# Two-branch gated attention on one core: the start of the projections, with all of x loaded at once and two q blocks taken per portion

## The chip, the cores and the metric

The kernel runs on one core of one Trainium2 chip. The metric is the device time of one execution in microseconds (us). Lower is better. Three runs of the kernel before gave 2798.04, 2798.07 and 2798.45 us, median 2798.07 us. One further execution was taken with the profiler.

## The reference, cut to what matters

Two attention blocks, A and B, see the same input `x` and have their own weights. A gate worked out from `x` mixes their outputs.

```python
# B = 1, S = 2048 tokens, D = 512, H = 32 heads, Dh = 16
def block(x, wqkv, wo):
    q, k, v = split_heads(x @ wqkv)                 # [D, 3D]: q, k, v
    p = softmax(q @ k.T * Dh ** -0.5)               # full, per head
    return merge_heads(p @ v) @ wo
g = sigmoid((x * gate_w).sum(-1, keepdims=True))
out = g * block(x, wqkv_a, wo_a) + (1 - g) * block(x, wqkv_b, wo_b)
```

The outermost part of this that matters here is `x @ wqkv`. It is done with every float32 operand split into a high part (rounded to the `float32r` format) and a low part (the rest), so that a product takes three matmuls: high by high, low by high, high by low.

## The kernel before, in words

The program is written engine by engine in a fixed order (`manual_schedule`): each engine takes its instructions in the order of the code, and waits on semaphores for what it reads and for buffers that must come free. The engines are TensorE (PE, with PEld for its weight loads), ScalarE (ACT), VectorE (DVE), GpSimd (POOL) and SyncE (SP), which issues nearly all DMAs.

The work falls in two stages.

1. **Projections**, about the first 300 us. `x` comes in transposed, `xT` [512, 2048], in four **portions** of 512 tokens. A portion is one tile `raw` of 128 x 4 x 512 float32 (1 MB): four pieces of 128 rows of `xT`, k = 0 to 3. `split_x` makes `xh` (ACT, a cast) and `xl` (DVE, a subtraction) from it; these stay for the whole stage. The columns of `wqkv` for q and k are taken in 16 **blocks** of 128 columns: for each branch s and each group g of 8 heads, one block of q and one of k. `load_w` fetches a block's weights (`wraw`, 256 KB, three buffers) and `split_w` makes `whi` (ACT) and `wlo` (DVE), two buffers each.
2. **Attention**, the other 2500 us: scores, row maxima, exponentials and sums for 64 heads, with the output projections between them. The change doesn't touch it.

`project_qk` works a block: for each of the four portions it makes one **tile** of 128 x 512 in a PSUM bank `ps_st` (four banks in rotation) by 12 matmuls (L251): `whi` by `xh` for k = 0 to 3, then `wlo` by `xh`, then `whi` by `xl`. ACT copies the tile's high part to `part0` (L254), DVE subtracts for `part1` (L255). Two tiles fill a `part` pair of 128 x 1024, two pairs in rotation. Two DMAs of 512 KB then write a pair to memory, to `qd` or `kd` (L257). For the first half of a k block, DVE and POOL work out a further remainder and SP writes it to `xd` (L261 to L267).

At the start, SP issues the first block's weights, the first portion in four pieces, the second portion in two, and the second block's weights. `raw` has two buffers, so the loads of the third and fourth portion (L230) stand on SP behind waits for the splits of the first and second (`split_x`, L236 on ACT and L237 on DVE). All four `split_x` stand on ACT and DVE ahead of the second block's `split_w` and of the first block's evictions. Then the blocks run one after the other: q of group 0, k of group 0, q of group 1, k of group 1, and so on. At the head of block i, SP gets the weights of block i + 3, and ACT and DVE split those of block i + 1.

`vpool` holds two tiles `vg` of 128 x 16 x 8 x 17 float32, each 2176 elements a partition, where a portion has 2048. They are first filled with v by `load_v` on POOL's queue, after block 9.

Of the kernel before, what the change touches and what calls it, by code (L numbers as in the profile page):

```python
# [51 lines left out]
def gated_mha(ctx: ExitStack, tc: tile.TileContext, xT, x, wqkv_a, wo_a, wqkv_b, wo_b, gate_w, out):  # L52
    nc = tc.nc
    pe, act, dve, pool = nc.tensor, nc.scalar, nc.vector, nc.gpsimd
# [7 lines left out]
    ps_st = ctx.enter_context(tc.tile_pool(name="ps_st", bufs=4, space=PSUM))  # L62
# [6 lines left out]
    xd = [[dram.tile([2, HG, DH, 512], F32, name=f"xd{s}{g}") for g in range(NG)] for s in range(2)]  # L69
# [111 lines left out]
    pt = {}  # L181
# [13 lines left out]
    vpool = ctx.enter_context(tc.tile_pool(name="vpool", bufs=2))  # L195
    vg = {}
# [9 lines left out]
    with tc.tile_pool(name="xs", bufs=1) as xs, tc.tile_pool(name="pro", bufs=2) as pro:  # L206
        xh = [xs.tile([P, KC, 512], F32R, name=f"xh{c}") for c in range(NQ)]
        xl = [xs.tile([P, KC, 512], F32R, name=f"xl{c}") for c in range(NQ)]
        wblocks = {}

        raws = {}

        def load_w(s, col, n):
            raw = pro.tile([P, KC, n], F32, name="raw" if n == 512 else "wraw", bufs=2 if n == 512 else 3)
            nc.sync.dma_start(raw, wqkv[s][:, col:col + n].rearrange("(k p) c -> p k c", p=P))
            raws[s, col] = raw

        def split_w(s, col, n):
            raw = raws.pop((s, col))
            tag, bufs = ("wv", 1) if n == 512 else ("w", 2)  # L220
            hi = pro.tile([P, KC, n], F32R, name=f"{tag}hi", bufs=bufs)
            lo = pro.tile([P, KC, n], F32R, name=f"{tag}lo", bufs=bufs)
            act.copy(hi, raw)
            dve.tensor_tensor(lo, raw, hi.bitcast(F32), op=ALU.subtract)
            wblocks[s, col] = (hi, lo)

        def load_x(c, n):
            raw = pro.tile([P, KC, 512], F32, name="raw")
            for k in range(0, KC, n):
                nc.sync.dma_start(raw[:, k:k + n], xT[k * P:(k + n) * P, c * 512:(c + 1) * 512].rearrange(  # L230
                    "(k p) t -> p k t", p=P))
            return raw

        def split_x(c, n, raw):
            for k in range(0, KC, n):
                act.copy(xh[c][:, k:k + n], raw[:, k:k + n])  # L236
                dve.tensor_tensor(xl[c][:, k:k + n], raw[:, k:k + n], xh[c][:, k:k + n].bitcast(F32),  # L237
                                  op=ALU.subtract)

        def project_qk(s, g, isk, between):  # L240
            hi, lo = wblocks.pop((s, isk * DM + g * P))
            dst = (kd if isk else qd)[s][g]
            for half in range(2):
                pt = [pro.tile([P, 1024], F32R, name=f"part{i}") for i in range(2)]
                for c in range(2):
                    cc = half * 2 + c
                    ps = ps_st.tile([P, 512], F32, name="ps_st")
                    n = 0
                    for a, b in ((hi, xh[cc]), (lo, xh[cc]), (hi, xl[cc])):
                        for k in range(KC):  # L250
                            pe.matmul(ps, a[:, k], b[:, k], start=n == 0, stop=n == 3 * KC - 1)  # L251
                            n += 1
                    sl = slice(c * 512, (c + 1) * 512)
                    act.copy(pt[0][:, sl], ps)  # L254
                    dve.tensor_tensor(pt[1][:, sl], ps, pt[0][:, sl].bitcast(F32), op=ALU.subtract)  # L255
                for i in range(2):
                    nc.sync.dma_start(dst[i].rearrange("h d t -> (h d) t")[:, half * 1024:(half + 1) * 1024],  # L257
                                      pt[i].bitcast(F32))
                if isk and half == 0:
                    d = pro.tile([P, 512], F32, name="rise_k", bufs=1)  # L260
                    dve.tensor_tensor(d, ps, pt[0][:, :512].bitcast(F32), op=ALU.subtract)  # L261
                    pool.tensor_tensor(d, d, pt[1][:, :512].bitcast(F32), op=ALU.subtract)
                    dt = [pro.tile([P, 512], F32R, name=f"rise_p{i}", bufs=1) for i in range(2)]
                    pool.tensor_copy(dt[0], d)
                    pool.tensor_tensor(dt[1], d, dt[0].bitcast(F32), op=ALU.subtract)
                    for i in range(2):
                        nc.sync.dma_start(xd[s][g][i].rearrange("h d t -> (h d) t"), dt[i].bitcast(F32))  # L267
                between()

        v_st = [const.tile([P, H, 17], F32, name=f"v_st{i}") for i in range(2)]  # L270
        for t in v_st:
            pool.memset(t[:, :, 16:17], 1.0)

        def project_v(s, t):
            hi, lo = wblocks[s, 2 * DM]
            c, o = divmod(t * P, 512)
            ps = ps_st.tile([P, 512], F32, name="ps_st")
            n = 0
            for a, b in ((xh[c], hi), (xl[c], hi), (xh[c], lo)):
                for k in range(KC):  # L280
# [12 lines left out]

        block(load_w, 0)
        x0 = load_x(0, 1)
        block(split_w, 0)
        split_x(0, 1, x0)
        for c in range(1, NQ):
            split_x(c, 2, load_x(c, 2))
            if c < 3:  # L300
                block(load_w, c)
        ahead = [(m, c) for m in range(NT + LEAD + 2) for c in range(4)]

        def run_ahead():
            turn[0] = 0
            for _ in range(min(3, len(ahead))):
                m, c = ahead.pop(0)
                max_plain(m, c)
                if (m, c) == (NT - 1, 3):
                    max_split(0)  # L310
                    pending.append(0)

        pending = []
        for i, (s, g, isk) in enumerate(blocks):
            block(split_w, i + 1)
            block(load_w, i + 3)
# [4 lines left out]
            project_qk(s, g, isk, run_ahead if i >= 8 else lambda: None)  # L321
# [136 lines left out]
    banks, fill_only = [], []  # L458
# [166 lines left out]
    for r in range(2, ROUNDS, 2):  # L625
        h, kt = divmod(r, NT)
# [69 lines left out]
```

## Time and profile before

| what | value |
|---|---|
| median of three runs | 2798.07 us (2798.04 to 2798.45) |
| profiled execution, its own time | 2798.53 us |
| its span, first to last instruction | 2796.8 us |
| mean granted TensorE clock | 0.999 |
| PE busy | 2781.7 us (99%) |
| ACT busy | 2424.0 us (87%) |
| DVE busy | 2363.1 us (84%) |
| POOL busy | 254.8 us (9%) |
| DMA, mean | 81 GB/s |

The span is 1.73 us shorter than the execution's own time: that much lies around the instructions. In the profile, `L251` is the line of the kernel that issued an instruction, `out<-in` names its tiles without their numbers, and `x4` says that four instructions of a kind are merged in a row. The busy time of a matmul is modelled and includes the time in which its results drain, so the pace of matmuls is read from their starts, not from their durations. "PE 98%" in the chain of work that ended last means that nearly all of the span is a chain of matmuls. The clock column gives the granted TensorE clock as a share of full speed.

### The profile page before, as it was taken

To read this page: it belongs to the slowest core of one execution; us is meant where nothing else is said; L and a number is where in the kernel's file an instruction comes from. 1 tells how busy PE (TensorE), PEld (TensorE's weight loads), DVE (VectorE), ACT (ScalarE), POOL (GpSimd) and SP (SyncE) were. 2 spreads that over 40 slices of the span, in tenths; PEclk is the share of its full clock that TensorE was granted. 3 is DMA by queue.
4 is the path that set the end of the run, shared out by engine and by line. 5 is a ranking of instruction groups with operands and counts; after the bars stand their busy time and mean duration, and the time that the engine had idled before them with its cause. 6 is when DMAs were issued, how large, how long until landed. Compare 5 with 4: busy or idle time off the path is not lost.

```text
span 2796.8 us, 65495 instructions
## 1 busy us (share of the span) xinstructions
PE 2781.7 (99%) x26176; PEld 1317.1 (47%) x26176; DVE 2363.1 (84%) x4431; ACT 2424.0 (87%) x4789; POOL 254.8 (9%) x456
## 2 busy tenths in 40 slices
PE   8999999999999999999999999999999999999999
PEld 7877544444444444444444445444444444444444
DVE  4155799999999999999999877899999999998774
ACT  3221799999999999999999977899999999998785
POOL 2010112110000000000100232000000001011201
PEclk9999999999999999999999999999999999999999
DMA  7673423333333223333432442332323333333302
GB/s 259 203 247 146 96 60 79 66 68 58 70 62 55 53 60 56 58 60 58 89 58 49 102 102 61 58 58 50 63 53 60 58 78 70 58 73 87 76 11 93
DMA packets 91126, 225.25 MB, mean 81 GB/s; under 512 B 24150, under 2 KB 34358, under 8 KB 78278
## 3 DMA queue, kind: packets, MB, share of 16 engines
q1 hardware_dynamic: 88262, 212.15, 34.0%
q0 software_dynamic: 2560, 8.91, 1.2%
q8 instruction: 206, 3.38, 0.5%
q14 instruction: 98, 0.80, 0.1%
HBM read 152.07 MB, written 68.94 MB: 79 GB/s over the span
## 4 chain that ended last, share of the span: by engine, by line
PE 98%; ACT 1%; DMA 0%; DVE 0%; SPq 0%; issue 0%
PE acc L589 38%; PE ps_m L140 26%; PE ps_st L191 13%; PE ps_st L140 8%; PE ps_st L251 6%; PE ps_st L281 3%; PE ps_m L475 3%; ACT p L193 1%; DMA raw<-in_xT 0%; PE ps_st L475 0%; PE ps_st L526 0%; PE ps_m L526 0%; DVE o_acc L527 0%; PE ps_m L513 0%; SPq L230 0%
## 5 line engine op out<-in xcount | busy, mean ns | idle before, releaser
L193 ACT ACTIVATE p<-ps_st 128x512 f32<-128x512 f32 x4088 | 2073.0, 626 | 82.7 <-PE ps_st L191 69.7
L145 DVE TENSOR_REDUCE mxp<-ps_m 128x1 f32<-128x512 f32 x3096 | 1949.8, 683 | 184.5 <-PE ps_st L191 135.2
L140 PE MATMUL ps_m<-k_st,q_st 48*128 48x512 f32 x3596 | 1353.9, 446 | 0.1
L191 PE MATMUL ps_st<-q_st,k_st 50*128 50x512 f32 x4096 | 1215.6, 426 | 0.0
L589 PE MATMUL acc<-p,vg 128*17 128x384 f32 (+1 forms) x16336 | 1182.8, 384 | 2.9 <-ACT ev L597 2.0
L140 PEld LDWEIGHTS ps_m<-k_st,q_st 48*128 48x128 f32 x3596 | 608.6, 183 | 550.0 <-DVE mxp L145 499.7
L191 PEld LDWEIGHTS ps_st<-q_st,k_st 50*128 50x128 f32 x4096 | 617.3, 184 | 200.3 <-ACT p L193 179.8
L589 PEld LDWEIGHTS acc<-p,vg 128*17 128x17 f32 x16336 | 313.9, 96 | 422.4 <-issue 399.6
L157 DVE CUSTOM_DVE_ANT_0 rise<-ps_m,rise 128x512 f32<-128x512 f32 x500 | 339.6, 679 | 0.0
L152 ACT ACTIVATE rise<-ps_st 128x512 f32<-128x512 f32 x500 | 301.8, 604 | 37.3
L140 PE MATMUL ps_st<-x_st,q_st 48*128 48x512 f32 x500 | 248.1, 496 | 0.0
L140 PEld LDWEIGHTS ps_st<-x_st,q_st 48*128 48x128 f32 x500 | 91.4, 183 | 211.6 <-ACT p L193 211.1
L167 POOL CAST mparts<-mrow 128x16 fp32r<-128x16 f32 x64 | 12.6, 197 | 1913.8 <-DVE mrow L166 1913.8
L254 ACT CAST part<-ps_st 128x512 fp32r<-128x512 f32 x64 | 37.4, 587 | 131.9 <-PE ps_st L251 117.0
L255 DVE TENSOR_TENSOR part<-ps_st,part 128x512 fp32r<-128x512 f32 x64 | 43.9, 690 | 90.3 <-ACT part L254 79.3
L475 PE MATMUL ps_m<-wo,ot 128*128 128x512 f32 (+1 forms) x354 | 91.0, 402 | 0.0
L284 ACT COPY v_st<-ps_st 128x512 f32<-128x512 f32 x32 | 18.8, 587 | 79.8 <-PE ps_st L281 70.3
L251 PE MATMUL ps_st<-xh,whi 128*128 128x512 f32 x256 | 73.0, 405 | 8.1 <-ACT xh L236 8.1
L475 PEld LDWEIGHTS ps_m<-wo,ot 128*128 128x128 f32 (+1 forms) x354 | 64.0, 188 | 20.3 <-DVE mxp L157 5.9
L251 PE MATMUL ps_st<-xh,wlo 128*128 128x512 f32 x256 | 69.9, 396 | 0.0
L251 PE MATMUL ps_st<-xl,whi 128*128 128x512 f32 x256 | 69.5, 394 | 0.0
L251 PEld LDWEIGHTS ps_st<-xh,whi 128*128 128x128 f32 x256 | 47.6, 191 | 24.7 <-ACT xh L236 10.4
(95 smaller groups left out, 814.4 us busy)
## 6 DMA issues: line engine op xcount, KB each, us to landing
k_st<-kd SPq DMA_DIRECT2D x128, 256.0 KB
q_st<-qd SPq DMA_DIRECT2D x128, 256.0 KB
qd<-part SPq DMA_DIRECT2D x32, 512.0 KB
kd<-part SPq DMA_DIRECT2D x32, 512.0 KB
k_st<-kd SPq DMA_DIRECT2D x128, 128.0 KB
q_st<-qd SPq DMA_DIRECT2D x128, 128.0 KB
od<-ev SPq DMA_DIRECT2D x63, 256.0 KB
vd<-v_st SPq DMA_DIRECT2D x32, 272.0 KB
```

Source lines behind the costliest of these rows:

```text
L140: pe.matmul(ps, q[b:b + SC, t * P:(t + 1) * P], k, start=True, stop=True)
L145: dve.tensor_reduce(o[:, c:c + 1], ps, op=ALU.max, axis=AX.X)
L152: act.activation(rises[m], ps, AF.Relu)
L157: dve.tensor_tensor_reduce(out=rise, in0=ps, in1=rise, scale=1.0, scalar=LOWEST, op0=ALU.add, op1=ALU.max, accum_out=o[:, 0:1])
L191: pe.matmul(ps, k[b:b + SC + 2, kk * P:(kk + 1) * P], q[b:b + SC + 2, cc * 512:(cc + 1) * 512], start=True, stop=True)
L193: act.activation(pt[r][:, c * 512:(c + 1) * 512], ps, AF.Exp, scale=SCALE)
L251: pe.matmul(ps, a[:, k], b[:, k], start=n == 0, stop=n == 3 * KC - 1)
L254: act.copy(pt[0][:, sl], ps)
L255: dve.tensor_tensor(pt[1][:, sl], ps, pt[0][:, sl].bitcast(F32), op=ALU.subtract)
L281: pe.matmul(ps, a[:, k, o:o + P], b[:, k], start=n == 0, stop=n == 3 * KC - 1)
L475: pe.matmul(ps, ot[a][:n, slot, sl], wt[b][:n, g], start=G == groups[0] and i == 0, stop=G == groups[-1] and i == 2)
L589: pe.matmul(acc[32 * c:32 * c + 17, qa * P:qb * P], v[:, 4 * a + c if final else kt, j], p[:, c * 512 + qa * P:c * 512 + qb * P], start=fi ...
```

## The change

Three things are changed at the start of the projections.

- **Loads.** `load_x` puts portions 0 and 1 into `raw` as before, and portions 2 and 3 into the two `vg` tiles of `vpool`. SP issues all of it ahead of anything else: the first block's weights, portion 0, the second block's weights, portions 1 to 3, the third block's weights. The weights of the fourth block, which SP issued ahead of the first write before, and those of the fifth now come after the writes of the first two blocks.
- **Order of the blocks.** The second and third change places: q of group 0, q of group 1, k of group 0, k of group 1, then as before.
- **Shared portions.** The first two blocks no longer run one after the other. For each portion, PE makes the tile of block 0 and that of block 1, ACT and DVE split the next portion, and then evict the two tiles. On portion 0, each of these two tiles goes piece by piece: for k = 0 to 3, high by high, low by high, high by low. The third block's `split_w` stands between the last evictions of the two blocks. `project_qk` is cut into `qk_tile` (matmuls) and `qk_parts` (eviction and writes); from the third block on they are called as before.

The diff, cut to its core:

```diff
         def load_x(c, n):
-            raw = pro.tile([P, KC, 512], F32, name="raw")
+            if c < 2:
+                raw = pro.tile([P, KC, 512], F32, name="raw")
+            else:
+                raw = vpool.tile([P, NT, HG, 17], F32, name="vg").rearrange("p k h d -> p (k h d)")
+                raw = raw[:, :KC * 512].rearrange("p (k t) -> p k t", k=KC)
...
+        PARTS = ((0, 0), (1, 0), (0, 1))
...
+        def qk_tile(i, cc):
...
+            steps = [(k, p) for k in range(KC) for p in PARTS] if cc == 0 and i < 2 else \
+                [(k, p) for p in PARTS for k in range(KC)]
+            for n, (k, (a, b)) in enumerate(steps):
+                pe.matmul(ps, w[a][:, k], (xh, xl)[b][cc][:, k], start=n == 0, stop=n == 3 * KC - 1)
+            return ps
...
         blocks = [(s, g, isk) for s in range(2) for g in range(NG) for isk in range(2)]
+        blocks[1:3] = blocks[2:0:-1]
...
         block(load_w, 0)
-        x0 = load_x(0, 1)
-        block(split_w, 0)
-        split_x(0, 1, x0)
-        for c in range(1, NQ):
-            split_x(c, 2, load_x(c, 2))
-            if c < 3:
-                block(load_w, c)
+        load_x(0, 1)
+        block(load_w, 1)
+        for c in range(1, NQ):
+            load_x(c, 2)
+        block(load_w, 2)
+        block(split_w, 0)
+        split_x(0, 1)
+        block(split_w, 1)
+        for c in range(NQ):
+            banks = [qk_tile(i, c) for i in range(2)]
+            if c < NQ - 1:
+                split_x(c + 1, 2)
+            qk_parts(0, c, banks[0])
+            if c == NQ - 1:
+                block(split_w, 2)
+            qk_parts(1, c, banks[1])
+        for i in (3, 4):
+            block(load_w, i)
...
-        for i, (s, g, isk) in enumerate(blocks):
+        for i in range(2, len(blocks)):
             block(split_w, i + 1)
             block(load_w, i + 3)
```

**SP's queue at the start.** `DMAHW0` and so on are the semaphores of DMAs, eight in rotation. A wait for one means that the DMA eight places earlier, or the one that the wait names by its semaphore, has landed; a wait for `DVE` is one for a split that frees a buffer. Before:

```order
L215 DMA wraw<-in_wqkv_a 128x4x128
L230 DMA raw<-in_xT 128x512 x4
L230 DMA raw<-in_xT 128x2x512 x2
L215 DMA wraw<-in_wqkv_a 128x4x128
L230 DMA raw<-in_xT 128x2x512 [waits DMAHW2_49,DMAHW3_49,DMAHW1_49,DMAHW4_49,DMAHW0_49,DVE_49]
L230 DMA raw<-in_xT 128x2x512
L215 DMA wraw<-in_wqkv_a 128x4x128
L230 DMA raw<-in_xT 128x2x512 [waits DMAHW6_49,DMAHW5_49,DVE_49]
```

Now:

```order
L215 DMA wraw<-in_wqkv_a 128x4x128
L234 DMA raw<-in_xT 128x512 x4
L215 DMA wraw<-in_wqkv_a 128x4x128
L234 DMA raw<-in_xT 128x2x512 x2
L234 DMA vg<-in_xT 128x2x512 [waits DMAHW0_49]
L234 DMA vg<-in_xT 128x2x512 [waits DMAHW1_49]
L234 DMA vg<-in_xT 128x2x512 [waits DMAHW2_49]
L234 DMA vg<-in_xT 128x2x512 [waits DMAHW3_49]
L215 DMA wraw<-in_wqkv_a 128x4x128 [waits DMAHW4_49]
```

The second block's weights moved ahead of portion 1, and the loads of portions 2 and 3 lost their waits for DVE; what they wait for is the landing of the first five loads.

**PE, the first tile.** Before, the four products with the high part of x stand first:

```order
L251 MATMUL ps_st<-xh_145,whi 128x512 x4
L251 MATMUL ps_st<-xh_145,wlo 128x512 x4
L251 MATMUL ps_st<-xl_149,whi 128x512 x4
L251 MATMUL ps_st<-xh_146,whi 128x512 x4
L251 MATMUL ps_st<-xh_146,wlo 128x512 x4
```

Now the first two pieces of portion 0 stand so, and two further pieces, then a whole second tile of the same portion, follow in the same way (`xh_145` and `xl_149` are portion 0, `xh_146` is portion 1):

```order
L255 MATMUL ps_st<-xh_145,whi 128x512 [waits Activation_49]
L255 MATMUL ps_st<-xh_145,wlo 128x512 [waits DVE_49]
L255 MATMUL ps_st<-xl_149,whi 128x512 [waits DVE_49]
L255 MATMUL ps_st<-xh_145,whi 128x512 [waits Activation_49]
L255 MATMUL ps_st<-xh_145,wlo 128x512
L255 MATMUL ps_st<-xl_149,whi 128x512 [waits DVE_49]
```

Three matmuls now follow each piece that arrives where one did, and 24 stand ahead of the first that reads portion 1 where 12 did.

**SP and ACT at the third block.** What SP issues behind the loads of x, now, from the first writes of block 0 and 1 (`qd_76` and `qd_77`) on:

```order
L271 DMA qd_77<-part_303 128x1024
L271 DMA qd_77<-part_304 128x1024
L215 DMA wraw<-in_wqkv_a 128x4x128 x3
L215 DMA raw<-in_wqkv_a 128x4x512
L271 DMA kd_84<-part_370 128x1024
```

and ACT's queue from the last evictions of blocks 0 and 1 to those of block 2 (`part_370`):

```order
L265 CAST part_299<-ps_st 128x512 [waits PE_49]
L223 CAST whi<-wraw 128x512 [waits DMAHW4_49]
L265 CAST part_303<-ps_st 128x512 [waits PE_49]
L223 CAST whi<-wraw 128x512 [waits DMAHW5_49]
L265 CAST part_370<-ps_st 128x512 [waits DMAHW1_49,DVE_49,PE_49]
L265 CAST part_370<-ps_st 128x512 [waits PE_49]
```

The second of the two casts of weights is that of block 3. Its load, which stood ahead of the first write before, now stands behind eight writes, and the cast stands ahead of all evictions of block 2. From block 3 on, the order of the instructions on PE, ACT, DVE and POOL is that of before.

More of the change, by code (lines that the diff above doesn't have):

```diff
@@ L231, in load_x, with split_x @@
                     "(k p) t -> p k t", p=P))
-            return raw
-        def split_x(c, n, raw):
+            raws[c] = raw
+        def split_x(c, n):
+            raw = raws.pop(c)
             for k in range(0, KC, n):
@@ L238, in split_x @@
                                   op=ALU.subtract)
-        def project_qk(s, g, isk, between):
-            hi, lo = wblocks.pop((s, isk * DM + g * P))
-            dst = (kd if isk else qd)[s][g]
[L243 to L268, printed above, removed]
@@ new lines, in gated_mha @@
+        PARTS = ((0, 0), (1, 0), (0, 1))
+        part = {}
+        def qk_tile(i, cc):
+            s, g, isk = blocks[i]
+            w = wblocks[s, isk * DM + g * P]
+            ps = ps_st.tile([P, 512], F32, name="ps_st")
+            steps = [(k, p) for k in range(KC) for p in PARTS] if cc == 0 and i < 2 else \
[3 more added lines that the diff above has]
+            return ps
@@ new lines, in qk_parts @@
+        def qk_parts(i, cc, ps):
+            s, g, isk = blocks[i]
+            half, c = divmod(cc, 2)
+            if c == 0:
+                part[i] = [pro.tile([P, 1024], F32R, name=f"part{j}") for j in range(2)]
+            pt = part[i]
+            sl = slice(c * 512, (c + 1) * 512)
+            act.copy(pt[0][:, sl], ps)
+            dve.tensor_tensor(pt[1][:, sl], ps, pt[0][:, sl].bitcast(F32), op=ALU.subtract)
+            if c == 0:
+                return
+            dst = (kd if isk else qd)[s][g]
+            for j in range(2):
+                nc.sync.dma_start(dst[j].rearrange("h d t -> (h d) t")[:, half * 1024:(half + 1) * 1024],
+                                  pt[j].bitcast(F32))
+            if isk and half == 0:
+                d = pro.tile([P, 512], F32, name="rise_k", bufs=1)
+                dve.tensor_tensor(d, ps, pt[0][:, :512].bitcast(F32), op=ALU.subtract)
+                pool.tensor_tensor(d, d, pt[1][:, :512].bitcast(F32), op=ALU.subtract)
+                dt = [pro.tile([P, 512], F32R, name=f"rise_p{j}", bufs=1) for j in range(2)]
+                pool.tensor_copy(dt[0], d)
+                pool.tensor_tensor(dt[1], d, dt[0].bitcast(F32), op=ALU.subtract)
+                for j in range(2):
+                    nc.sync.dma_start(xd[s][g][j].rearrange("h d t -> (h d) t"), dt[j].bitcast(F32))
@@ L270, in gated_mha, with project_qk @@
+        def project_qk(i, between):
+            for cc in range(NQ):
+                qk_parts(i, cc, qk_tile(i, cc))
+                if cc % 2:
+                    between()
         v_st = [const.tile([P, H, 17], F32, name=f"v_st{i}") for i in range(2)]
@@ L320, in gated_mha @@
                 split_w(i // 8, 2 * DM, DM)
-            project_qk(s, g, isk, run_ahead if i >= 8 else lambda: None)
+            project_qk(i, run_ahead if i >= 8 else lambda: None)
             if i in (5, 6, 8, 9):
```

## The prediction

> **What bounds the kernel now.** I read the page's head and its chain first, then who PE waited for.
>
> ```profile
> span 2796.8 us, 65495 instructions
> PE 98%; ACT 1%; DMA 0%; DVE 0%; SPq 0%; issue 0%
> ```
>
> The chain that ended last is PE's own work. The view of PE's waits over the whole span has three rows:
>
> ```profile
> PE ps_st L251 <- ACT xh L236: 8.1, 5, 5.8
> PE acc L589 <- ACT ev L597: 2.0, 3, 0.7
> PE acc L589 <- ACT ev L606: 0.9, 1, 0.9
> ```
>
> So PE waits 8.1 us for the splits of x, 5.8 us of it ahead of its first matmul, and 2.9 us in all the rest. What PE saves at the start ends the program earlier by as much, as long as no new wait comes in between. PE's timeline at the start shows where the time goes (start, modelled duration, count, idle time before):
>
> ```profile
> 5.80 0.80 PE L251 MATMUL ps_st<-xh,whi 128*128 128x512 f32 x1 [5.80 <-ACT xh L236]
> 7.16 1.47 PE L251 MATMUL ps_st<-xh,whi 128*128 128x512 f32 x2 [0.57 <-ACT xh L236]
> 8.86 0.79 PE L251 MATMUL ps_st<-xh,whi 128*128 128x512 f32 x1 [0.23 <-ACT xh L236]
> 9.45 1.91 PE L251 MATMUL ps_st<-xh,wlo 128*128 128x512 f32 x4
> 11.16 1.29 PE L251 MATMUL ps_st<-xl,whi 128*128 128x512 f32 x4
> 12.29 1.07 PE L251 MATMUL ps_st<-xh,whi 128*128 128x512 f32 x4
> ...
> 16.08 0.73 PE L251 MATMUL ps_st<-xh,whi 128*128 128x512 f32 x2 [0.91 <-ACT xh L236]
> 17.44 0.73 PE L251 MATMUL ps_st<-xh,whi 128*128 128x512 f32 x2 [0.63 <-ACT xh L236]
> ...
> 24.20 1.07 PE L251 MATMUL ps_st<-xh,whi 128*128 128x512 f32 x4
> ...
> 35.08 1.07 PE L251 MATMUL ps_st<-xh,whi 128*128 128x512 f32 x4
> ```
>
> By starts there are two paces. From 24.20 to 35.08 lie 48 matmuls in 10.88 us: **0.227 us** each. From 9.45 to 11.16 lie four in 1.71 us: **0.428 us** each. The group at 11.16 takes 1.13 us, which is 1.1 matmuls at the slow pace and 2.9 at the fast one, so the pace changed at about 11.6 us. The windows show the other slow stretch as a granted clock of one half:
>
> ```profile
> 4.74:8.15 3.41, 1.79 (x3) 0.86 (x3) 2.11 (x4) 1.85 (x3) 3.32 (x3) 1.00 0.94 302
> 8.15:11.56 3.41, 3.18 (x7) 2.15 (x7) 1.52 (x3) 1.82 (x3) 0.77 (x3) 1.00 0.98 318
> 14.98:18.39 3.41, 1.87 (x7) 1.11 (x7) 2.19 (x2) 2.09 (x2) 0.00 (x0) 1.00 1.03 330
> 18.39:21.80 3.41, 3.41 (x10) 2.66 (x9) 2.30 (x3) 2.94 (x4) 0.00 (x0) 0.50 0.32 101
> ```
>
> (Bounds, their length, busy time of PE, PEld, DVE, ACT and POOL, clock, DMA share, GB/s.) The clock was halved for 3.41 us after a stretch in which PE stood idle for 0.91 and 0.63 us. Ahead of 11.6 us the column says 1.00 though the starts say half; there the pace counts. The steps fit a grid of 3.41 us: 11.56, 14.98, 18.39, 21.80.
>
> **The account of before.** Matmul 97, the first of the third block, starts at 35.08. The 96 ahead of it would take 96 x 0.227 = 21.76 us at the fast pace, from 5.80 to 27.56. So 7.52 us are lost: the slow pace at the start, the idle times between portions, and the halved clock. The change can win this sum and no more.
>
> **The start after the change.** The first weights and portion 0 are issued as before, so PE starts at 5.80. What the splits do is in ACT's timeline:
>
> ```profile
> 3.81 0.62 ACT L223 CAST whi<-wraw 128x512 fp32r<-128x512 f32 x1 [1.79 <-DMA wraw<-in_wqkv_a]
> ...
> 6.49 1.29 ACT L236 CAST xh<-raw 128x512 fp32r<-128x512 f32 x2 [0.75 <-DMA raw<-in_xT]
> 8.19 0.62 ACT L236 CAST xh<-raw 128x512 fp32r<-128x512 f32 x1 [0.41 <-DMA raw<-in_xT]
> 10.01 1.04 ACT L236 CAST xh<-raw 128x1024 fp32r<-128x1024 f32 x1 [1.21 <-DMA raw<-in_xT]
> 11.40 1.05 ACT L236 CAST xh<-raw 128x1024 fp32r<-128x1024 f32 x1 [0.34 <-DMA raw<-in_xT]
> 14.98 1.04 ACT L236 CAST xh<-raw 128x1024 fp32r<-128x1024 f32 x1 [2.54 <-DMA raw<-in_xT]
> 16.34 1.05 ACT L236 CAST xh<-raw 128x1024 fp32r<-128x1024 f32 x1 [0.31 <-DMA raw<-in_xT]
> 18.46 1.04 ACT L236 CAST xh<-raw 128x1024 fp32r<-128x1024 f32 x1 [1.07 <-DMA raw<-in_xT]
> 19.91 1.04 ACT L236 CAST xh<-raw 128x1024 fp32r<-128x1024 f32 x1 [0.40 <-DMA raw<-in_xT]
> ```
>
> and in DVE's:
>
> ```profile
> 5.78 0.69 DVE L237 TENSOR_TENSOR xl<-raw,xh 128x512 fp32r<-128x512 f32 x1 [0.63 <-ACT xh L236]
> 7.14 1.37 DVE L237 TENSOR_TENSOR xl<-raw,xh 128x512 fp32r<-128x512 f32 x2 [0.67 <-ACT xh L236]
> 8.84 0.69 DVE L237 TENSOR_TENSOR xl<-raw,xh 128x512 fp32r<-128x512 f32 x1 [0.33 <-ACT xh L236]
> 12.48 1.23 DVE L237 TENSOR_TENSOR xl<-raw,xh 128x1024 fp32r<-128x1024 f32 x1 [0.16 <-ACT xh L236]
> ```
>
> Each piece now feeds three matmuls, 1.28 us at the slow pace. Piece 0 (its low part ready at 6.47): 5.80 to 7.08. Piece 1 is split at 7.11 and runs from 7.16 to 8.44, piece 2 (7.78 and 8.51 for the two parts) to 9.73, piece 3 (8.81 and 9.53) to 11.01. PE no longer waits within the portion. The second tile of portion 0 starts at 11.01. By 11.56 it has done 1.3 matmuls; the other 10.7 take 2.43 us, so the two tiles end at **13.99**. If all six tiles of portions 1 to 3 follow without a wait, matmul 97 starts 72 x 0.227 = 16.32 us later, at **30.31**.
>
> **What must be there by then.** The bound for each load comes from the landings above, which are the ends of ACT's waits. Two halves of a portion land 1.36 to 1.45 us apart (14.98 to 16.34, 18.46 to 19.91); with a block of weights between them it is 2.12 (16.34 to 18.46). So weights cost **about 0.7 us** of the queue.
> - The second block's weights: after 8.19, and before the 10.01 of the larger transfer that stood in this place; I take 9.3, nearer to 8.19 + 0.7. Split on ACT (0.62) and DVE (0.69), they are ready at 10.6, at worst 11.3. PE wants the low part at 11.44.
> - Portion 1: 0.7 later than before, so its second half lands at 12.1 and is split at 13.15; wanted at 14.44. At the slowest spacing, 2.12 us for each half, it would land at 13.5 and be split at 14.5: 0.1 us late.
> - Portions 2 and 3: at 1.4 us a half, 13.5, 14.9, 16.3 and 17.7. ACT comes to portion 2 after the evictions of portion 0, at 14.8, and ends at 16.9; wanted from 19.43. ACT comes to portion 3 after those of portion 1, at 20.2, and ends at 22.3; wanted from 24.87. DVE ends them about 1.5 us later, and its parts are wanted eight matmuls, 1.8 us, later than ACT's.
> - Evictions, at the durations of these rows:
>
> ```profile
> 24.40 0.59 ACT L254 CAST part<-ps_st 128x512 fp32r<-128x512 f32 x1 [1.47 <-PE ps_st L251]
> 25.02 0.69 DVE L255 TENSOR_TENSOR part<-ps_st,part 128x512 fp32r<-128x512 f32 x1 [0.41 <-ACT part L254]
> ```
>
>  A bank is wanted again four tiles later, 10.9 us; the evictions of a pair of tiles, with the split of a portion ahead of them, take 2 x 1.04 + 2 x 0.59 = 3.3 us of ACT and 2 x 1.23 + 2 x 0.69 = 3.8 us of DVE out of 5.44 us of PE. They hide.
> - The third block's weights: its buffers come free at the end of block 0's last tile, 27.59; with the eviction ahead of it ACT has `whi` at 28.8, DVE `wlo` at 29.7. PE wants them at 30.31 and 31.2. They hide, though only by 1.5 us.
>
> **Writes and the fourth block's weights.** The same bytes are written, but in bursts of four DMAs, and the load of block 3's weights stands behind them. SP's rows of before bound it, with the cast that used the weights of its row at 26.11:
>
> ```profile
> 22.47 3.59 SPq L257 DMA_DIRECT2D qd<-part  x4
> 26.11 0.87 SPq L215 DMA_DIRECT2D wraw<-in_wqkv_a  x1
> ...
> 35.76 0.62 ACT L223 CAST whi<-wraw 128x512 fp32r<-128x512 f32 x1
> ```
>
> A load right behind four writes had landed at most 9.65 us after its issue. The last write of block 1 waits for DVE at 31.8, so this load goes out at 32.3 and lands at 41.9 at the latest. PE wants the split weights at 30.31 + 10.88 = 41.19. From above that is a wait of 41.9 + 0.62 - 41.19 = 1.3 us. From below it is nothing: the cast at 35.76 waited for no DMA. I take nothing, since four writes of 512 KB and the weights, 2.36 MB, need 7.1 us at the 330 GB/s of the window from 14.98: landed at about 39.5. ACT holds block 2's evictions until then, and four banks cover it.
>
> Portions 2 and 3 sit in `vg`; POOL's first load of v into them, hundreds of instructions later, finds them long free: nothing. The order of q and k moves no work of PE.
>
> **The sum.** 35.08 - 30.31 = 4.77 us less. Against the profiled execution's 2798.53 us (its span and 1.73 us around it) that is 2793.76; the median of the runs is 0.46 us lower, so **2793.3 us**, a gain of 0.17%. A measurement of this kernel can tell about 0.2%, 5.6 us, from no change, so this falls within 0.2%.
>
> [...] The four times of before lie within 0.49 us, which speaks for a grid that stands still.
>
> **Rivals.**
> 1. *The full clock comes one window earlier, at 8.15.* The stretch from 4.74 to 8.15 held 2.8 matmuls at the slow pace before (1.2 us, 35%) and stayed slow; now it holds 5.3 (2.27 us, 66%). The stretch from 14.98 with about 1.5 us of matmuls (43%) led to the half clock, that from 8.15 with 2.8 us (82%) to the full one, so 66% lies between. Then the first tile ends at 9.8, and the second waits for its weights: high part 9.97, low part 10.68, and eleven matmuls, to 13.17. The gain is 5.6 us, **2792.5**; with weights landing at 8.9 it is 6.0. The limit is the whole 7.52 us, 2790.6.
> 2. *A wait is left, and the clock falls again.* If portion 1 lands late or the grid lies so that a window holds a wait, PE loses the wait, some 0.5 us, and a halved window, 3.41 x 0.5 = 1.7 us. Gain 2.6 us, **2795.5**. For it: 0.1 us at the bound above, and DMA shares of 0.94 to 1.03. Against it: margins of 1.3 us or more at the likely spacing, and no wait in tiles that have 24 matmuls ahead of them.
> 3. *Slower: the fourth block's weights come too late.* ACT stands at this cast, evictions of block 2 stop behind it, and PE stops at 41.19. Each microsecond that the weights land after 40.5 is lost. From 40.5 + 4.8 = 45.3 the change is slower than before; 4 us beyond that, with one halved window of 1.7 us, it is 2798.1 + 5.7 = **2803.8**. Before, this landing was within 9.65 us of its issue; for this it would have to take 17.
> 4. *The change doesn't do what it says: the loads still come one by one.* Portions 2 and 3 wait on SP for the first four landings. These lie between 3.81 and 8.19, ahead of the queue's turn. Even with the old landings, 14.98 to 19.91, and 0.7 us more for each, portion 2 is split at 18.1 (wanted at 19.43) and portion 3 at 21.7 (wanted at 24.87). So the time is the forecast's, **2793.3**: with 24 matmuls for each portion, it is not the early loads alone that remove the waits.
>
> **How the numbers follow.** Forecast (4.2 to 5.2 us gained), rival 4 among it, 60%; rival 1 22%; rival 2 13%; rival 3 5%. The range goes from rival 1 with room for earlier weights, 2791.6, to just beyond rival 2, 2796.2; it leaves out rival 3 and the outer ends of the two others, some 15% in all. Rival 1's time lies at the 5.6 us that count as faster: most of it and a little of the forecast give 20% for faster; 75% is for the same and 5% for slower.
>
> **What would show it.** Right: PE's waits for x fall from 8.1 to about 5.9 us, no row of the clock column says 0.50 after 12 us, the pace changes at 11.6, and the 97th matmul starts at 30.3. ACT's first eviction comes at about 13, and ACT waits once for the fourth block's weights without a wait of PE at 41. Wrong: a pace that changes at 8.2 (rival 1), an idle row on PE between 11 and 25 (rival 2), or PE waiting for `wraw` or a bank between 38 and 60 (rival 3). A gain at 30 us that isn't there at the end of the span would upset the premise that PE's chain carries it through.

## The result, and the profile after

| | before | after |
|---|---|---|
| median, 20 runs each | 2798.01 us | 2793.26 us |
| lowest to highest | 2797.43 to 2798.91 | 2792.18 to 2794.87 |
| profiled execution, its own time | 2798.53 | 2794.23 |
| its span | 2796.8 | 2792.4 |

The ratio is 0.9983, with a 95% interval of 0.9977 to 0.9989: 4.75 us or 0.17% less. The forecast was 2793.3 us, and within 0.2% of before.

PE's waits over the whole span of the kernel after (total, times, longest); the first three rows answer to the three of before, and the fourth is one wait in the attention stage:

```profile
PE ps_st L255 <- ACT xh L241: 6.2, 2, 5.7
PE acc L621 <- ACT ev L629: 2.0, 3, 0.7
PE acc L621 <- ACT ev L638: 0.9, 1, 0.9
PE ps_st L140 <- ACT p L193: 0.5, 1, 0.5
```

Of the 8.1 us of waiting for x, 6.2 are left, 5.7 of them ahead of the first matmul. PE's timeline, from its first matmul to the first of the third block, which is matmul 97:

```profile
5.75 0.79 PE L255 MATMUL ps_st<-xh,whi 128*128 128x512 f32 x1 [5.75 <-ACT xh L241]
6.34 0.63 PE L255 MATMUL ps_st<-xh,wlo 128*128 128x512 f32 x1
6.76 0.63 PE L255 MATMUL ps_st<-xl,whi 128*128 128x512 f32 x1
7.87 0.80 PE L255 MATMUL ps_st<-xh,whi 128*128 128x512 f32 x1 [0.48 <-ACT xh L241]
...
9.32 0.63 PE L255 MATMUL ps_st<-xh,whi 128*128 128x512 f32 x1
...
11.02 0.57 PE L255 MATMUL ps_st<-xh,wlo 128*128 128x512 f32 x1
11.43 0.40 PE L255 MATMUL ps_st<-xl,whi 128*128 128x512 f32 x1
11.67 0.40 PE L255 MATMUL ps_st<-xh,whi 128*128 128x512 f32 x1
...
14.40 1.07 PE L255 MATMUL ps_st<-xh,whi 128*128 128x512 f32 x4
...
30.72 1.07 PE L255 MATMUL ps_st<-xh,whi 128*128 128x512 f32 x4
```

From 14.40 to 30.72 lie 72 matmuls in 16.32 us, 0.227 us each: PE never waits in portions 1 to 3, and its pace does not fall again. Matmul 97 starts at 30.72 instead of 35.08, 4.36 us earlier. The span is 4.4 us shorter, and what follows matmul 97 takes 2796.8 - 35.08 = 2761.7 us before and 2792.4 - 30.72 = 2761.7 us after. So all of the gain is made in the first 31 us, and none is lost behind them.

ACT's timeline shows what PE had to wait for, and what it did not:

```profile
7.20 2.00 ACT L241 CAST xh<-raw 128x512 fp32r<-128x512 f32 x3 [1.51 <-DMA raw<-in_xT]
9.40 0.62 ACT L223 CAST whi<-wraw 128x512 fp32r<-128x512 f32 x1 [0.20 <-DMA wraw<-in_wqkv_a]
10.74 1.05 ACT L241 CAST xh<-raw 128x1024 fp32r<-128x1024 f32 x1 [0.72 <-DMA raw<-in_xT]
12.10 1.06 ACT L241 CAST xh<-raw 128x1024 fp32r<-128x1024 f32 x1 [0.31 <-DMA raw<-in_xT]
...
15.08 2.00 ACT L241 CAST xh<-vg 128x1024 fp32r<-128x1024 f32 x2
...
37.86 0.62 ACT L223 CAST whi<-wraw 128x512 fp32r<-128x512 f32 x1 [6.36 <-DMA wraw<-in_wqkv_a]
```

The second piece of x was split from 7.20 instead of 6.49, and PE waited for it: 0.48 us in the view, whose durations are modelled, and 0.7 us by the starts (1.11 us from 6.76 to 7.87, where the pace is 0.43). Portion 1 landed at 10.74 and 12.10. ACT found portion 2 there when it came to it at 15.08. It stood for 6.36 us for the fourth block's weights.

### The profile page after: what moved, and what is told of

Its sections match the earlier page's. It is cut to its first block, busy times and chain, and to the rows that moved or that the text cites. A ratio compares the mean times of both kernels' runs of the same rounds, so it can differ in the third digit from the quotient of the medians.

```text
span 2792.4 us, 65494 instructions
## 1 busy us (share of the span) xinstructions
PE 2778.9 (100%) x26176; PEld 1316.1 (47%) x26176; DVE 2363.5 (85%) x4431; ACT 2423.8 (87%) x4789; POOL 255.9 (9%) x456
## 4 chain that ended last, share of the span: by engine, by line
PE 98%; ACT 1%; DMA 0%; DVE 0%; issue 0%; SPq 0%
PE acc L621 38%; PE ps_m L140 26%; PE ps_st L191 13%; PE ps_st L140 8%; PE ps_st L255 6%; PE ps_st L300 3%; PE ps_m L507 3%; ACT p L193 1%; PE ps_st L507 0%; PE ps_st L558 0%; DMA raw<-in_xT 0%; PE ps_m L558 0%; DVE o_acc L559 0%; PE ps_m L545 0%; ACT ev L629 0%
```

## The experiments

Each kernel was timed against the kernel before on the same chip. The theory was that two tiles for each portion, taken piece by piece in portion 0, fill PE, and that every later wait is covered. The rival was that the early loads of portions 2 and 3 bring the gain.

### One part at a time

**The old loads, the rest of the change kept** (`e1_old_loads`). All portions go through the two `raw` buffers.

```diff
...
-        for c in range(1, NQ):
-            load_x(c, 2)
-        block(load_w, 2)
+        load_x(1, 2)
         block(split_w, 0)
         split_x(0, 1)
+        load_x(2, 2)
...
                 split_x(c + 1, 2)
+            if c == 0:
+                load_x(3, 2)
+                block(load_w, 2)
```

> The change with its loads undone: all four portions go through the two raw buffers again, so that the loads of portions 2 and 3 wait for the splits of portions 0 and 1. Theory (two tiles for each portion fill PE): portion 2 lands some 5 us after the split of portion 0, at about 15 and 16.5 us, portion 3 at 19 and 20.5; PE wants them at 19.8 and 25.3. PE doesn't wait, matmul 97 starts at 30.3 to 30.7, and the time is that of the change, 2793.3 us (within 0.5). Rival (the early loads bring the gain): PE waits as before for portions 2 and 3, and the time goes back to 2796 to 2798 us.

Measured: 2793.51 us (2792.99 to 2794.84; ratio 0.9985, 0.9976 to 0.9994). SP's timeline shows the loads of portions 1 to 3 drawn out until 15.2 us:

```profile
3.68 11.49 SPq L230 DMA_DIRECT2D raw<-in_xT  x6
```

PE's waits over the span have one row for x:

```profile
PE ps_st L251 <- ACT xh L237: 6.0, 1, 6.0
```

And in PE's timeline matmul 97 starts no later than in the change:

```profile
30.13 1.07 PE L251 MATMUL ps_st<-xh,whi 128*128 128x512 f32 x4
```

So the only wait for x that the view gives is the one ahead of PE's first matmul, and the early loads add nothing to the shared portions.

**The early loads alone** (`e2_loads_only`). The kernel before, with portions 2 and 3 in `vg` and issued at once.

```diff
...
-        x0 = load_x(0, 1)
+        xr = [load_x(0, 1)]
+        for c in range(1, NQ):
+            xr.append(load_x(c, 2))
+            if c < 3:
+                block(load_w, c)
         block(split_w, 0)
-        split_x(0, 1, x0)
+        split_x(0, 1, xr[0])
         for c in range(1, NQ):
-            split_x(c, 2, load_x(c, 2))
-            if c < 3:
-                block(load_w, c)
+            split_x(c, 2, xr[c])
```

> The kernel before with only the loads of the change: portions 2 and 3 go to the vg tiles and are issued at once, and the blocks run one after the other as before. Theory: portion 2 is split at about 16 and portion 3 at 19.5; PE waits 0.5 and 1 us instead of 0.9, 0.6 and a halved clock, matmul 97 starts at 32.6, and the time is 2795.5 us, about half of the gain. Rival (the early loads bring the gain): 2793.3 us.

Measured: 2796.88 us (2796.39 to 2798.27; ratio 0.9996, 0.9987 to 1.0004), 1.4 us less than before in the medians, and the interval holds no change. The time is 1.4 us above the expected 2795.5, and matmul 97 started at 33.39 and not at 32.6. PE still waits for portions 2 and 3, in the middle of their first tile:

```profile
16.29 0.74 PE L255 MATMUL ps_st<-xh,whi 128*128 128x512 f32 x2 [0.33 <-ACT xh L240]
...
19.89 0.73 PE L255 MATMUL ps_st<-xh,whi 128*128 128x512 f32 x2 [0.59 <-ACT xh L240]
...
33.39 1.07 PE L255 MATMUL ps_st<-xh,whi 128*128 128x512 f32 x4
```

The portions were split where expected, but 12 matmuls (2.7 us) are done before the next portion is split, 3.6 us later. The loads alone are worth less than half of the change. The shared portions with neither the early loads nor the order by pieces were not run by themselves.

**The order by pieces undone** (`e3_parts_first`).

```diff
-            steps = [(k, p) for k in range(KC) for p in PARTS] if cc == 0 and i < 2 else \
-                [(k, p) for p in PARTS for k in range(KC)]
+            steps = [(k, p) for p in PARTS for k in range(KC)]
```

> The change with the order within the tiles of portion 0 undone: four products of the high parts, then the others. Theory: PE waits for the pieces within the first tile as before, this tile ends at 12.3 and the second at 15.0 instead of 14.0 to 14.4; matmul 97 starts at 31.3, 0.6 to 1.0 us later, time 2794.1 us. Rival (the slow pace until 11.5 hides the order): no difference, 2793.3 us.

Measured: 2795.35 us (2794.14 to 2796.67; ratio 0.999, 0.9981 to 0.9999), 2.1 us above the change where 0.8 was expected. PE's timeline at the start:

```profile
7.18 2.43 PE L254 MATMUL ps_st<-xh,whi 128*128 128x512 f32 x3 [0.56 <-ACT xh L241]
9.40 1.91 PE L254 MATMUL ps_st<-xh,wlo 128*128 128x512 f32 x4
11.11 1.91 PE L254 MATMUL ps_st<-xl,whi 128*128 128x512 f32 x4
12.82 1.24 PE L254 MATMUL ps_st<-xh,whi 128*128 128x512 f32 x4
13.89 1.09 PE L254 MATMUL ps_st<-xh,wlo 128*128 128x512 f32 x4
```

The group at 12.82 takes 1.07 us, 0.8 matmuls at the slow pace and 3.2 at the fast one, so here the pace changed at 13.2 us, not at 11.4. The second tile ends at 15.72. The stretch of 3.41 us that ended at 9.7 held four starts, 1.6 us of matmuls at 0.43 us each, 47% of it, and the pace stayed slow. Matmul 97 came at 32.05, 1.3 us later than in the change, and two things make this up. By 9.4 us PE has started five matmuls, where the change starts its seventh at 9.32: two fewer, 0.5 us at the fast pace. And the slow pace lasts 1.7 us longer, which costs 0.8 us. The first is what the order by pieces does to the waits. That the order also brings the fast pace sooner is argued from one profile of each kernel: in two executions of the change itself the pace changed at 11.4 and at 8.4 us (`after_again`, below).

**The old order of the blocks** (`e7_q_then_k`): the two blocks that share the portions are q and k of group 0.

```diff
-        blocks[1:3] = blocks[2:0:-1]
```

> The change with the old order of the blocks: the two that share the portions are q and k of group 0. Theory (PE has the same matmuls; the remainder of k adds 0.7 us to DVE and 3.2 to POOL beside 5.4 us of PE): 2793.3 us within 0.5. Rival (both have to be q, since the remainder delays evictions or writes): PE waits for a bank or part between 19 and 31 us, 2794 us or more.

Measured: 2792.87 us (2792.18 to 2794.9; ratio 0.9982, 0.9973 to 0.999). Matmul 97 started at 30.05, and PE's one wait for x is that of the start (5.6 us). That both blocks are q makes no difference that can be seen.

### The wait for the fourth block's weights

**Loaded still later** (`e4_w3_late`): behind the weights of two more blocks and the 1 MB of v's weights.

```diff
-        for i in (3, 4):
-            block(load_w, i)
+        for i in (4, 5):
+            block(load_w, i)
+        load_w(0, 2 * DM, DM)
+        block(load_w, 3)
...
```

> The change with the weights of the fourth block loaded still later, behind those of the fifth and sixth and the 1 MB of v's weights. Theory (four banks cover ACT's wait up to the start of the fourth block): the weights land at 42 to 42.5 us instead of 37.9, PE wants them at 41.6 and also needs the bank that ACT and DVE evict behind them, so PE stands from 41.6 to about 44, 2 to 3 us, and if the clock is halved after that 1.7 us more: 2795.5 to 2798 us. Rival (ACT's wait has no such limit near by): 2793.3 us.

Measured: 2798.17 us (2797.3 to 2800.17; ratio 0.9999, 0.9991 to 1.0008): the whole gain is gone. In ACT's timeline, the cast of these weights:

```profile
42.80 0.62 ACT L223 CAST whi<-wraw 128x512 fp32r<-128x512 f32 x1 [11.55 <-DMA wraw<-in_wqkv_a]
```

In PE's, the start of the fourth block:

```profile
44.80 1.51 PE L255 MATMUL ps_st<-xh,whi 128*128 128x512 f32 x4 [3.29 <-DVE part L266]
46.11 1.91 PE L255 MATMUL ps_st<-xh,wlo 128*128 128x512 f32 x4
```

And the windows around it (PE, PEld, DVE, ACT, POOL, clock, DMA share, GB/s):

```profile
42.09:45.50 3.41, 0.70 (x3) 0.61 (x4) 2.04 (x4) 2.69 (x6) 0.00 (x0) 1.00 0.08 32
45.50:48.91 3.41, 3.41 (x10) 2.63 (x9) 2.36 (x4) 0.39 (x1) 2.73 (x3) 0.50 0.69 276
```

The weights came 4.9 us later than in the change. PE stood for 3.29 us, waiting in the end for the bank that the held-up eviction freed, and then ran for 3.41 us at half the clock (0.50 in the row from 45.50 to 48.91), which costs 1.7. Together that is 5.0 us, and the median is 4.9 above the change's. This is the prediction's third rival, brought about by the edit: it has its price. If each microsecond of delay of the cast delays PE by as much, the cast that just costs nothing starts 3.29 us earlier, at 39.5. By this estimate the wait begins to cost when the weights land 1.7 us later than in the change.

**Loaded early** (`e5_w3_early`): right behind the loads of x.

```diff
         block(split_w, 0)
+        block(load_w, 3)
         split_x(0, 1)
...
-        for i in (3, 4):
-            block(load_w, i)
+        block(load_w, 4)
```

> The change with the weights of the fourth block loaded right behind the loads of x. Theory (ACT's wait of 6.4 us for them is covered by four banks): the wait goes away, PE's work doesn't move, 2793.3 us within 0.5. Rival (evictions that come late cost PE something already): 0.5 to 1 us faster.

Measured: 2792.91 us (2792.64 to 2794.87; ratio 0.9983, 0.9974 to 0.9991). ACT makes the cast at 31.11 and waits only for PE's tiles from then on:

```profile
31.11 0.63 ACT L223 CAST whi<-wraw 128x512 fp32r<-128x512 f32 x1
33.35 0.59 ACT L265 CAST part<-ps_st 128x512 fp32r<-128x512 f32 x1 [1.61 <-PE ps_st L255]
```

A wait of 6.4 us on ACT went away and the time stayed, within what can be told: the four banks had covered it.

### The slow pace at the start

In the profile after, matmul 97 starts 30.72 - 5.75 = 24.97 us after the first, 3.2 us more than 96 x 0.227. Four kernels ask how much of it can be won.

**Extra matmuls ahead of the first** (`e6_warm`), and **the same with more of them while the pieces land** (`e9_warm_fill`). They multiply the identity matrix into a bank that nobody reads.

```diff
+        warm = ps_m.tile([P, 512], F32, name="ps_m")
+        for i in range(40):
+            pe.matmul(warm[:, :P], ident, ident, start=True, stop=True)
```

> The change with 40 extra matmuls of 128 columns on the identity matrix, into a bank that nobody reads, ahead of the first real one, so that PE is busy from about 1.4 to 5.7 us. Nothing of the computation is left out. Theory (of the 3.2 us that are still lost by matmul 97, 2.5 are the slow pace): the pace changes by 8.2 us, the second tile of portion 0 is then bound by the second block's weights (low part ready at 10.7) and ends at 13.2 instead of 14.4; matmul 97 starts at 29.5, time 2792.3 us. Rival (the slow pace isn't set by PE's own activity): no change, or slower by what the extra matmuls reach beyond 5.75 us.

> The change with 40 extra matmuls of 128 columns ahead of the first real one, six more behind the three of the first piece and three behind those of the second, so that PE has no pause while the pieces land; nothing of the computation is left out. [...] Rival (the extra matmuls cost what they win): 2793.2 us.

**Both tiles of portion 0 piece by piece in turn**, six matmuls for each piece, with the second block's weights loaded behind the first piece (`e8_pieces`), and **the same with extra matmuls** (`e10_pieces_fill`).

```diff
...
+            for k in range(KC):
+                for i in range(2):
+                    s, g, isk = blocks[i]
+                    w = wblocks[s, isk * DM + g * P]
+                    for n, (a, b) in enumerate(PARTS):
+                        pe.matmul(ps[i], w[a][:, k], (xh, xl)[b][0][:, k], start=k + n == 0,
+                                  stop=k == KC - 1 and n == 2)
...
```

> The change with both tiles of portion 0 taken piece by piece in turn, six matmuls for each piece, the second block's weights loaded behind the first piece, and the halves of portion 1 taken one after the other. Theory: PE has six matmuls where it had three while pieces land, ends the two tiles of portion 0 some 1 to 2 us earlier (12.4 to 13.4), since the pace changes as before at 10 to 13 us but fewer matmuls are left for then; portion 1 is split at 13.2 and may cost 0.3 us: 2792 us. Rival (the slow pace binds, not the arrival): 24 matmuls at the slow pace until it changes are the same in any order, 2793.3 us.

> As the run before it, but with both tiles of portion 0 taken piece by piece in turn, the second block's weights loaded behind the first piece, and portion 1 by halves. Theory (with the full pace the arrival binds, so the order that failed at the slow pace now pays): the two tiles end at about 12, matmul 97 starts at 28.6, median 2791.3 us. Rival (the order by pieces costs time at any pace): 2793 us or more.

**The change once more**, on the chip of `e9_warm_fill` and `e10_pieces_fill` (`after_again`).

> The change itself once more, beside the other two on the same chip. Theory (the grid of the clock runs free of the program): the pace changes at another time than 11.4 us, anywhere from 9.2 to 12.6, matmul 97 starts up to 0.7 us earlier or later than 30.7, and the median is 2793.3 us within 0.3. Rival (the grid stands still): 11.4 us again.

| kernel | median (lowest to highest) | ratio to before (95%) | matmul 25 | matmul 97 |
|---|---|---|---|---|
| `e6_warm` | 2792.87 (2791.7 to 2794.62) | 0.9982 (0.9973 to 0.9991) | 12.91 | 29.23 |
| `e8_pieces` | 2794.03 (2793.13 to 2795.41) | 0.9984 (0.9975 to 0.9993) | 14.69 | 31.01 |
| `e9_warm_fill` | 2794.70 (2794.17 to 2795.36) | 0.998 (0.9971 to 0.9988) | 12.83 | 29.15 |
| `e10_pieces_fill` | 2795.04 (2794.65 to 2795.79) | 0.9981 (0.9972 to 0.999) | 13.23 | 29.55 |
| `after_again` | 2795.37 (2794.86 to 2796.7) | 0.9982 (0.9973 to 0.9991) | 13.43 | 29.75 |

Matmuls are counted without the extra ones. The last three ran on a chip where the kernel before took 2800.48 us, 2.2 us more than beside the others, so they compare among themselves. The difference lies behind the start: from matmul 97 to the end their profiles have 2763.7 us, 2.0 more than the change's 2761.7. There the change gained 5.1 us, `e10_pieces_fill` 5.4 and `e9_warm_fill` 5.8. The last is 0.7 us below the change in the median, a fortieth of a percent, and six of its eleven runs lie below the change's lowest, though the ranges overlap and the intervals against before do as well. `e6_warm` had the start that was expected in its profile (29.23 for 29.5), yet its median equals that of `e5_w3_early` and `e7_q_then_k`, which ran beside it without extra matmuls. A gain of 1 us there is not shown.

PE's timeline of `e9_warm_fill` shows what is left once the pace is fast:

```profile
1.36 4.45 PE L322 MATMUL ps_m<-ident 128*128 128x128 bf16 x40 [1.36 <-POOL ident masks.py:199]
...
5.57 0.78 PE L255 MATMUL ps_st<-xh,whi 128*128 128x512 f32 x1
...
8.39 0.47 PE L255 MATMUL ps_st<-xh,whi 128*128 128x512 f32 x1
8.70 0.39 PE L255 MATMUL ps_st<-xh,wlo 128*128 128x512 f32 x1
8.93 0.40 PE L255 MATMUL ps_st<-xl,whi 128*128 128x512 f32 x1
...
9.85 0.40 PE L255 MATMUL ps_st<-xh,whi 128*128 128x512 f32 x1
10.21 0.50 PE L255 MATMUL ps_st<-xh,wlo 128*128 128x512 f32 x1
12.83 1.07 PE L255 MATMUL ps_st<-xh,whi 128*128 128x512 f32 x4
```

The matmuls at 8.70 and 8.93 are 0.23 us apart, the fast pace. From 5.57 to matmul 97 at 29.15 are 23.58 us, 1.8 more than 96 x 0.227. Of these, 1.5 lie ahead of 8.39, in the six matmuls of the first two pieces: 0.5 in the two that start before 6.51, while the pace changes, and 1.0 where the extra matmuls fill the time until the next part of x is split. Another 0.2 lie about the second tile's weights: 9.85 is its first matmul, 10.21 the first with their low part, 0.36 us later where the pace is 0.23.

`e8_pieces` and `e10_pieces_fill` missed what was expected of them. For `e8_pieces`, the theory failed, as matmul 25 came at 14.69 and not before 13.4, and the rival's "no difference" isn't seen either: the median is 1.1 us above those of `e5_w3_early` and `e7_q_then_k` beside it. PE's waits have a new row, for the second block's weights:

```profile
PE ps_st L268 <- ACT whi L223: 0.4, 1, 0.4
```

In `e10_pieces_fill` matmul 25 comes 7.31 us after the first matmul of x, and in `e9_warm_fill` 7.26. So with the fast pace the order by pieces in turn neither won nor lost; the first matmul itself came 0.35 us later, at 5.92. The medians are 0.3 us apart, with ranges that overlap.

The rows that settle a point of the prediction are in `after_again`:

```profile
5.40 0.80 PE L255 MATMUL ps_st<-xh,whi 128*128 128x512 f32 x1 [5.40 <-ACT xh L241]
...
8.12 0.53 PE L255 MATMUL ps_st<-xh,whi 128*128 128x512 f32 x1
8.49 0.39 PE L255 MATMUL ps_st<-xh,wlo 128*128 128x512 f32 x1
8.72 0.40 PE L255 MATMUL ps_st<-xl,whi 128*128 128x512 f32 x1
...
10.17 0.40 PE L255 MATMUL ps_st<-xh,whi 128*128 128x512 f32 x1
10.80 0.50 PE L255 MATMUL ps_st<-xh,wlo 128*128 128x512 f32 x1 [0.23 <-DVE wlo L224]
...
13.43 1.07 PE L255 MATMUL ps_st<-xh,whi 128*128 128x512 f32 x4
```

The same program that changed pace at 11.4 us did so at 8.4 here (0.37 us from 8.12 to 8.49, 0.23 to 8.72). This is the prediction's first rival, with its wait for the second block's weights, in one execution of the change itself. The expectation put the change of pace between 9.2 and 12.6, and matmul 97 within 0.7 us of 30.7; both came earlier still.

Two things differ between the two executions. The change of pace lies 3.0 us earlier. By an estimate with steps of the clock 3.41 us apart, as in the profile of before (18.39 to 21.80), they shifted only a little: 8.4 and 3.41 more is 11.8, 0.4 us from 11.4. And the second piece of x was split from 5.54 here and from 7.20 there, so that PE went on without a pause. Counted as starts at 0.43 us each, the stretch of 3.41 us that ended at 8.4 held 2.9 us of matmuls (84%), and the one that ended at 8.0 in the profile after 1.45 us (42%). A start without a pause did not always bring an early change: in `e7_q_then_k` PE didn't pause either, and the pace changed at 11.05, 5.4 us after the first matmul, where it was 3.0 us in `after_again`:

```profile
5.61 0.79 PE L255 MATMUL ps_st<-xh,whi 128*128 128x512 f32 x1 [5.61 <-ACT xh L241]
...
10.90 0.46 PE L255 MATMUL ps_st<-xh,whi 128*128 128x512 f32 x1
11.20 0.40 PE L255 MATMUL ps_st<-xh,wlo 128*128 128x512 f32 x1
```

At 7.64, 3.41 us ahead of that change, PE had run for only 2.0 us, 1.9 us (55%) in the same count, and the pace stayed slow.

## Why the prediction was right, point by point

- **The bound and the carry-through** held. PE's chain takes 2761.7 us from matmul 97 on, before and after. In the profiles of the first eight experiments, leaving out `e4_w3_late`, it is 2761.2 to 2761.9.
- **The start.** 13.99 was forecast for the end of portion 0's tiles, 14.40 came. The pace was right (0.42 us from 6.34 to 6.76, 0.24 from 11.43 to 11.67), and so was the time of its change (11.6 forecast, 11.4 measured). What failed is the step "PE no longer waits within the portion". The second piece of x landed 0.7 us later than in the profile of before, which cost 0.7 us by the starts. Besides, the first matmul behind each of the two waits takes 0.59 us and not 0.43 (5.75 to 6.34; 7.87 to 8.46). The first tile ended at 11.67 and not at 11.01. The second won 0.25 of this back, as all of it ran at the fast pace.
- **The 72 matmuls behind it** took 16.32 us, as forecast, so matmul 97 came at 30.72 for 30.31.
- **The landings.** The price of 0.7 us for a block of weights in the queue gave 12.1 for the second half of portion 1, and 12.10 came; that it is so close is luck, as in the other profiles with this order of loads up to there it was 11.7 to 12.5. The second block's weights were forecast at 9.3 and came at 9.40. ACT's first eviction was forecast at about 13 and came at 13.06.
- **The fourth block's weights** were estimated to land at about 39.5, with a bound of 41.9, and landed at 37.86; PE did not wait. The third rival's point was too late: by the estimate from `e4_w3_late` PE loses time from a cast at 39.5 on, not from 40.5, since it waits not only for the weights but for the bank that is evicted behind their cast. The margin in the change was 1.7 us by the same estimate, and at the prediction's bound of 41.9 PE would have lost some 2.4 us and not 1.3.
- **Where the gain is from.** The prediction's fourth rival said that with 24 matmuls for each portion the early loads are not what removes the waits. `e1_old_loads` shows it.
- **What was wrong: the grid that stands still.** The prediction took the four times of before, 0.49 us apart, as a sign that the clock's steps fall at the same time in each execution. The runs speak against it. The pace changed at 10.3 us in `e1_old_loads`, at 12.4 in `e2_loads_only` and at 13.2 in `e3_parts_first`, on one chip and less than 3.41 us apart, where the prediction's grid of 3.41 us, standing still, would put them whole steps apart; and at 11.4 and 8.4 in two executions of the change, 3.0 us apart (on two chips, as the 2.0 us behind matmul 97 suggest). A grid within one execution rests on two profiles: steps at 11.6, 18.39 and 21.80 before, and at 11.4, 45.50 and 48.91 in `e4_w3_late`, in each some whole multiple of 3.41 us apart. No run shows the limits of 9.2 and 12.6 us in the expectation of `after_again`: in the profiles without extra matmuls the pace changed between 8.4 and 13.2. In five profiles of kernels with the change's order (`after`, `after_again`, `e1_old_loads`, `e5_w3_early`, `e7_q_then_k`) matmul 97 starts between 29.75 and 30.72 us. The 20 runs of the change lie 2.7 us apart, and those of before 1.5; how much of that is the clock's was not measured.
- **The number owes something to luck.** The sum was 0.41 us too early for matmul 97. The step from the profiled execution to the median, 0.46 us in the forecast, was 0.97. The two misses cancel, and 2793.3 meets the median of 2793.26 more closely than its terms do.
- **Left open:** how the chance of an early change of pace depends on the order of the matmuls over many executions. Of each kernel but the change, with two, only one execution was profiled.

## What to carry to other kernels

At a start that waits for data, count how many matmuls each arriving piece feeds: when a piece feeds more work than the next one takes to arrive, the loads need not be any earlier. Read the pace of matmuls from their starts (0.43 and 0.227 us here), and look behind a stretch in which PE is half idle for a halved clock: here 3.41 us of it came after 38 to 43% of matmuls (before) and after 20% (`e4_w3_late`). A wait on an engine beside the bound was free here only up to a point (6.36 us on ACT cost nothing, 11.55 us cost 4.9): find the buffer that covers it, and how far the point is.

## What the runs showed of the hardware that was not expected

The clock fell without a stretch that was idle throughout. Before, the stretch from 14.98 to 18.39 had no pause longer than 0.91 us and held 1.3 to 1.5 us of matmuls (38 to 43%), and 3.41 us at half the clock followed it (0.50 from 18.39 to 21.80). In `e4_w3_late` 3.41 us at 0.50 followed a stretch with 20% (0.70 us of modelled busy time from 42.09 to 45.50).

Ahead of the changes to the fast pace at the start PE was busier than that. The stretches here are counted back from the change of pace by 3.41 us, and the matmuls in them as starts at 0.43 us each. The pace stayed slow after 42% (the change), 47% (`e3_parts_first`) and 55% (`e7_q_then_k`). It became fast after 78% (before, from 8.15; the prediction has 82%, as it counts the first matmul behind a wait up to the next start) and after 84% (`after_again`). The stretch of `after_again` in the profile's modelled busy time is 2.99 of 3.42 us:

```profile
4.97:8.39 3.42, 2.99 (x7) 2.39 (x8) 2.29 (x4) 1.61 (x3) 3.33 (x3) 1.00 0.88 285
```

By that measure the stretch of `e3_parts_first` that ended at 9.7 has 2.74 us (80%), and the pace stayed slow behind it. So slow and fast lie apart in both counts, at 55% and 78% in the one and at 80% and 88% in these two rows of the other; that a share of busy time decides was not shown.
